# Block-sparse attention and a gated feed-forward on one Trainium2 core: the written order of arithmetic changed past the third pair of ff tiles of batch 0

## The chip, the cores and the metric

The kernel runs on one core of one Trainium2 chip, in one launch. The core has five engines that work side by side, each through its own list of instructions in order: TensorE (PE, matmuls; its weight loads are shown apart as PEld), VectorE (DVE), ScalarE (ACT), GpSimd (POOL) and SyncE (SP). POOL and SP here also issue the transfers between HBM and the on-chip memories: loads of q, k, v and the weights go out on POOL's queue, stores, DMA transposes and small on-chip copies on SP's. The metric is the device time in microseconds of one execution; less is better.

## The reference

Two stages, one behind the other. The first is attention with a band and block summaries: q, k and v have 4 batches of 8 heads of 768 rows of 64. The second is a gated feed-forward on the 3072 x 512 result.

```python
k_sum = k.reshape(B, H, 24, 32, D).max(axis=3)      # one key per block of 32
v_sum = v.reshape(B, H, 24, 32, D).mean(axis=3)
scores_l = q @ k.T / 8                              # only where |i - j| < 16
scores_s = q @ k_sum.T / 8 + log(32)                # all 24 blocks
a = softmax(concat([scores_l masked, scores_s]))
x = a @ concat([v, v_sum])                          # -> 3072 x 512
h = x @ w_in                                        # 512 x 2048
out = (h * sigmoid(1.702 * h)) @ w_out              # 2048 x 512
```

Inputs and output are float32.

## The kernel before

**Tiles.** A batch is 768 tokens. Its eight heads are four pairs (a pair fills 128 partitions), its tokens two halves of 384. Attention works on pairs; the feed-forward's first product makes 16 tiles of 128 ff rows for each half, its second three pieces of 128 rows for each half, and these by seven block products in place of eight, from sums of the GELU's outputs (`gs`) and of the weights (`ws`).

**What sets the order.** Nothing is left to a scheduler. A long string, `ORDER` (lines 35 to 111), holds 1,002 words `name.arguments`; lines 932 to 934 look each word up in `ops` (line 916) and call it, in the order of the string. A wrapper, `_Ordered` (lines 18 to 32), keeps the instructions of each engine in that program order, which is why every instruction bears line 28 in the profile. So a word fixes the place of its instructions on their engine, and the engines are tied together only by the semaphores that the tiles' reads and writes call for. An instruction that waits holds back all that follow it on its engine, DMA issues on POOL and SP among them.

**The words that matter here.**

- Loads on POOL: `lk`, `lq`, `lv` (a pair's keys or queries, a part of the values), into `kb`, `qb` and `vw`. `gate.b` (line 910) is a small POOL copy that holds the loads behind it until the block sums of the batch before have landed in `vw`, or, for the last batch, the turned `x`.
- Keys and queries of batch 1: `tk`, `tq` turn them on PE (`ps_t`), `kc`, `qc` copy them out, `kh` copies the neighbours' rows (halos), `xm` takes the block maxima, `kr` puts them in rows of `kx`. Batches 2 and 3 are turned by DMA transposes on SP instead (`xk`, `xq`), and then `xa` (maxima of two pairs, DVE), `ka` (line 420, halos, POOL or DVE) and `kR` (line 428, maxima into rows of `kx`, DVE) follow.
- Attention: `s.b.half.p` scores into a pair of PSUM banks (PE, `ps_s`), `e` exp (ACT), `m` the mask (DVE), `vm` the block sums of the values on PE, `vb` (line 373) the same on DVE, `sd` and `ha` (lines 345 and 336) copies of the sums and halos into `vw` on SP, `v` the values (PE, `ps_av`), `nn` the division (DVE, `x`). `t` and `c` turn `x` on PE and copy it; in later batches `d` does it by a DMA transpose on SP.
- Feed-forward: `f.half.nt.kos.bank` (line 722) one ff tile of 4 matmuls into a PSUM bank (`ph`), `g` (line 738) its GELU on ACT, which frees the bank; `gs.j.n.what` (line 741) the sums of GELU outputs, on DVE or with `.g` on POOL; `ws` (line 819) the same of weights; `p.t.what.bank` (line 830) one product of 8 matmuls (`poA`, `poB`, `poC`); `x.t.what` (line 853) takes it from the bank by a copy or an addition into an output buffer (`osb`); `o.b.t.half` (line 870) the store on SP. `G` and `X` load ACT's tables for GELU and for exp.

**Buffers.** There are eight PSUM banks: 0 to 3 for ff tiles, products and sums, and 4 and 5 of two banks each, named by halves (40, 41, 50, 51). There are three output buffers `osb`: a fourth piece can be started only when a store has landed. `vw`, `kx` and `qT` have two sets each.

**Stages.** While the ff tiles of batch b run on PE and the GELU on ACT, keys and values of batch b+1 come in and are made ready; the products of batch b then stand between the scores, exps and values of batch b+1. Half 1 of an ff tile needs all tokens of half 1, so the ff stage of a batch begins with the tiles whose tokens are ready.

Of the kernel before, what the change touches and what calls it, by code (L numbers as in the profile page):

```python
# [43 lines left out]
f.0.2.k0123.1 s.0.1.3.42 e.1.3 f.0.1.k23 f.0.4.k0123.50 mf f.0.6.k0123.40 f.0.5.k0123.51 f.0.7.k0123.41 G  # L44
f.0.3.k0123.0 g.0.2 g.0.0 g.0.1 g.0.4 g.0.6 g.0.3 lk.1.3 lq.1.0 g.0.7 g.0.5 lq.1.3 ck.1 m.1.0 m.1.2 ow.1 lk.1.4 lk.1.1
lk.1.2 lv.1.5.1 lk.1.5 lk.1.6 lq.1.2 lk.1.7 m.1.1 lq.1.1 lv.1.0.0 lq.1.4 lq.1.5 lq.1.7 lv.1.3.1 lq.1.6 lv.1.0.1
lv.1.2.0 lv.1.1.0 cv.1 lv.1.1.1 lv.1.4.0 lv.1.2.1 f.0.8.k0123.2 lv.1.4.1 late m.1.3 ws.0.0 g.0.8 f.0.9.k0123.3
# [35 lines left out]
o.1.2.0.0.2 p.2.4 x.2.4.a f.0.1.k01.0 f.0.9.k01.3 f.0.0.k01.2 f.0.0.k23 xk.1.1.0 xk.1.0.1 f.0.8.k01.1 f.0.8.k23
f.0.1.k23 lv.3.5.1 lq.3.1 lq.3.2 g.0.0 g.0.8 g.0.1 o.1.1.1.0.2 f.0.9.k23 g.0.9 xk.1.1.1 xk.1.0.0 o.1.2.1.0.2 xq.1.1
f.1.0.k0123.2 g.1.0 f.1.8.k0123.1 g.1.8 f.1.1.k0123.0 xq.1.0 g.1.1 gs.0.2.2 f.1.9.k0123.3 g.1.9 f.0.2.k0123.2 g.0.2
f.1.2.k0123.1 g.1.2 f.0.10.k0123.0 gs.0.2.0.d gs.0.2.1 gs.0.2.3 g.0.10 f.1.10.k0123.3 g.1.10 xa.0.1 f.1.3.k0123.1
f.0.3.k0123.2 g.0.3 f.1.11.k0123.3 f.0.11.k0123.0 g.1.3 gs.2.2.2.g g.0.11 g.1.11 ka.1.d gs.2.2.0 f.0.12.k0123.1
ha.3.3.0 f.0.4.k0123.2 gs.2.2.1.g g.0.12 g.0.4 f.1.12.k0123.3 ha.3.1.0 g.1.12 vm.3.52 f.1.4.k0123.0 vb f.1.14.k0123.3
g.1.14 sd.3.1.0 f.0.5.k0123.2 g.1.4 ha.3.0.0 ha.3.2.0 xa.1.1 gs.2.2.3 kR.1.d g.0.5 f.1.5.k0123.1 f.1.13.k0123.3 g.1.5
g.1.13 f.0.13.k0123.0 gs.4.2.0 gs.4.2.2 g.0.13 gs.4.2.1 gs.4.2.3 f.0.6.k0123.2 g.0.6 f.1.6.k0123.1 g.1.6  # L90
f.0.14.k0123.0 g.0.14 gs.6.1.0 gs.6.1.2 gs.6.1.1 gs.6.1.3 sd.3.0.0 f.0.7.k0123.2 g.0.7 f.1.7.k0123.1 g.1.7
f.0.15.k0123.0 g.0.15 f.1.15.k0123.3 g.1.15 gs.7.1.0 p.0.1.2 x.0.1.d p.0.5.1 gs.7.1.1.g s.3.0.0.52 X s.3.0.1.42 e.0.1
# [872 lines left out]
```

## Time and profile before

| | |
|---|---|
| runs of before, us | 212.35, 213.48, 214.64; median 213.48 |
| the profiled execution, us | span 212.3; its own time is not listed apart from this span |
| PE busy | 199.1 (94%), 2440 matmuls |
| DVE, ACT, POOL busy | 127.8 (60%), 117.7 (55%), 108.6 (51%) |
| granted PE clock | full in all 40 slices |
| POOL's queue / SP's queue, share of the 16 DMA engines | 85.7% / 31.9% |
| chain that ended last | PE 72%, DMA 18%, POOL 4%, issue 2%, DVE 1% |

The span counts from the first to the last recorded event of one execution. A group of instructions is named output<-input by the program's tiles, so `ph<-xT,w_in_sb` is an ff tile, `poA`, `poB` and `poC` are products, `ps_s` scores, `ps_av` values, `ps_t` turns and `gT<-ph` the GELU. A row of the timeline gives start, duration, engine, operation, tiles and shapes, the number of instructions drawn together, and in brackets the idle time ahead with what ended it. A row of the waits gives engine, tile, what released it, then total idle us, number of times and the longest in us. A row of the chain gives start, duration, engine, tile and number of instructions. A row of the windows gives the stretch, its length, then for each engine the busy time and the number of instructions: PE, PEld, DVE, ACT, POOL; behind them the granted clock, the DMA share and GB/s. A row of the DMA issues gives tiles, queue, operation, count, size and the median time from issue to landing.

### The profile page before, as it was taken

To read this page: it belongs to the slowest core of one execution; us is meant where nothing else is said; L and a number is where in the kernel's file an instruction comes from. 1 tells how busy PE (TensorE), PEld (TensorE's weight loads), DVE (VectorE), ACT (ScalarE), POOL (GpSimd) and SP (SyncE) were. 2 spreads that over 40 slices of the span, in tenths; PEclk is the share of its full clock that TensorE was granted. 3 is DMA by queue.
4 is the path that set the end of the run, shared out by engine and by line. 5 is a ranking of instruction groups with operands and counts; after the bars stand their busy time and mean duration, and the time that the engine had idled before them with its cause. 6 is when DMAs were issued, how large, how long until landed. Compare 5 with 4: busy or idle time off the path is not lost.

```text
span 212.3 us, 5885 instructions
## 1 busy us (share of the span) xinstructions
PE 199.1 (94%) x2440; PEld 145.3 (68%) x2440; DVE 127.8 (60%) x311; ACT 117.7 (55%) x227; POOL 108.6 (51%) x157
## 2 busy tenths in 40 slices
...
PEclk9999999999999999999999999999999999999999
...
GB/s 69 156 166 190 209 218 216 178 135 123 98 138 203 111 160 179 120 164 170 145 153 201 134 220 128 253 171 59 3 99 60 181 112 0 0 3 0 99 102 99
DMA packets 96458, 27.74 MB, mean 131 GB/s; under 512 B 85024, under 2 KB 93488, under 8 KB 96432
## 3 DMA queue, kind: packets, MB, share of 16 engines
q0 software_dynamic: 70800, 13.64, 85.7%
q1 hardware_dynamic: 25632, 13.74, 31.9%
...
## 4 chain that ended last, share of the span: by engine, by line
PE 72%; DMA 18%; POOL 4%; issue 2%; DVE 1%; SPq 0%; POOLq 0%
PE ph L28 31%; PE poA L28 19%; PE poB L28 9%; DMA w_out_sb<-in_moe_w_out_dram 7%; PE poC L28 5%; DMA kb<-in_k_dram 4%; DMA v0n<-in_v_dram 4%; DMA vw<-vs 3%; PE ps_av L28 3%; PE ps_s L28 2%; PE ps_t L28 1%; POOL kb L28 1%; PE ps_vs L28 1%; DVE vs L28 1%; POOL mk L28 1%
## 5 line engine op out<-in xcount | busy, mean ns | idle before, releaser
L28 PE MATMUL ph<-xT,w_in_sb 128*128 128x384 f16 x512 | 85.9, 326 | 0.0
L28 ACT ACTIVATE gT<-ph 128x384 f16<-128x384 f32 x128 | 58.7, 495 | 22.9 <-PE ph L28 21.9
L28 PEld LDWEIGHTS <-w_in_sb 128*128 128x128 f16 x512 | 49.2, 98 | 31.5 <-DMA w_in_sb<-in_moe_w_in_dram 0.2
L28 PEld LDWEIGHTS <-gs 128*128 128x128 f16 x384 | 36.3, 98 | 4.7
L28 DVE TENSOR_TENSOR gs<-gT 128x768 f16<-128x768 f16 (+1 forms) x36 | 17.1, 490 | 21.5 <-ACT gT L28 21.4
L28 PEld LDWEIGHTS <-gT 128*128 128x128 f16 x288 | 27.5, 98 | 3.7
L28 ACT ACTIVATE a_sb<-ps_s 128x768 bf16<-128x768 f32 x32 | 24.5, 808 | 9.1 <-PE ps_s L28 9.0
...
L28 PE MATMUL poA<-ws,gs 128*128 128x256 f16 x192 | 24.9, 273 | 0.0
L28 POOL TENSOR_TENSOR gs<-gT 128x768 f16<-128x768 f16 x4 | 6.9, 1728 | 35.0 <-ACT gT L28 35.0
L28 ACT ACTIVATE s<-poA 128x256 f32<-128x256 f32 x14 | 5.4, 384 | 20.6 <-PE poA L28 19.0
L28 DVE TENSOR_TENSOR x<-ps_av,rc 128x768 f16<-128x768 f32 (+1 forms) x18 | 15.6, 869 | 0.6
L28 DVE TENSOR_TENSOR a_sb<-a_sb,mk 128x768 bf16<-128x768 bf16 x28 | 14.6, 549 | 1.8 <-ACT a_sb L28 1.1
L28 POOL TENSOR_TENSOR gs<-gs,gT 128x768 f16<-128x768 f16 (+1 forms) x6 | 8.4, 1406 | 12.9 <-DVE gs L28 12.9
L28 DVE TENSOR_TENSOR gs<-gT,gs 128x768 f16<-128x768 f16 (+1 forms) x19 | 9.2, 490 | 7.2 <-POOL gs L28 6.6
L28 PE MATMUL poB<-ws,gs 128*128 128x256 f16 x96 | 12.5, 273 | 0.0
L28 PE MATMUL poB<-w_out_sb,gs 128*128 128x256 f16 x96 | 12.5, 273 | 0.0
L28 PE MATMUL poA<-ws,gT 128*128 128x256 f16 x96 | 12.5, 273 | 0.0
L28 PE MATMUL poC<-w_out_sb,gT 128*128 128x256 f16 x96 | 12.5, 273 | 0.0
L28 PE MATMUL poA<-w_out_sb,gT 128*128 128x256 f16 x96 | 12.3, 273 | 0.0
...
## 6 DMA issues: line engine op xcount, KB each, us to landing
out_dram<-osb SPq DMA_DIRECT2D x23, 256.0 KB, 2.9
...
```

Source lines behind the costliest of these rows:

```text
L28: r = f(*a, **kw)
```

## The change

Only the `ORDER` string differs. Its 1,002 words are the same, in another sequence, and the two strings are equal up to `g.0.11`, the GELU of ff tile 11 of half 0 in batch 0; `v.0.1.2.50` follows soon in both, and what comes behind it is in another order. Loads on POOL's queue keep their sequence among each other, as do the transfers on SP's, but for one store at the end; the arithmetic between them has moved, so a given load or store can stand ahead of an instruction that it stood behind before. Bank and engine are part of a word, so over the whole string each is used as often as before.

The core of the diff, by stage. Second half of the ff tiles of batch 0 with the keys of batch 1, and the first products:

```diff
...
-c.1.1.d f.1.0.k01.2 f.1.8.k01.3 f.1.1.k0123.1 ws.1.0 g.0.15 g.1.1 f.1.0.k23 ws.2.0 f.1.8.k23 g.1.0 g.1.8 ws.0.1 ws.1.1
-f.1.9.k0123.0 g.1.9 gs.0.2.0 ws.3.0 gs.0.2.1 gs.0.2.3 f.1.10.k0123.1 gs.0.2.2 ws.2.1 g.1.10 f.1.2.k0123.3 g.1.2
-f.1.3.k0123.2 g.1.3 f.1.11.k0123.1 g.1.11 gs.2.2.0 gs.2.2.1 gs.2.2.2 f.1.12.k0123.3 gs.2.2.3 g.1.12 f.1.4.k0123.2
-tk.0.52 kc.0.a f.1.13.k0123.0 g.1.13 ws.3.1 g.1.4 f.1.5.k0123.1 g.1.5 tk.1.52 gs.4.2.2 kc.1.a f.1.14.k0123.3 tk.2.42
...
-s.1.1.1.52 e.1.1 m.0.1 vm.1.42 vb sd.1.1.0 kr.2.1.g kh.3.1.d sd.1.0.0 xm.3.1 kr.3.1.d p.1.5.1 gate.1 lv.2.3.0 lv.2.1.1
...
-lq.2.7 o.0.1.0.0.2 v.1.0.0.50 m.1.3 v.1.0.1.51 p.1.4 x.1.4.a o.0.1.1.0.2 p.2.5.1 x.2.5.a m.0.3 v.1.1.0.40 v.1.1.1.41
...
+v.0.1.3.51 nn.1.1 f.0.15.k0123.0 g.0.12 f.0.14.k0123.1 g.0.13 t.1.1.52 c.1.0.d c.1.1.d g.0.15 ws.0.1 g.0.14 f.1.8.k01.3
+f.1.0.k01.2 f.1.8.k23 ha.1.3.0 f.1.9.k0123.0 f.1.0.k23 ws.1.1 g.1.8 g.1.9 f.1.1.k0123.1 ws.2.0 f.1.2.k0123.3 g.1.0
+f.1.3.k0123.2 g.1.1 ws.1.0 gs.0.2.0 ha.1.2.0 f.1.10.k0123.1 g.1.3 gs.0.2.1 f.1.4.k0123.2 g.1.2 gs.2.2.2 g.1.10 lv.1.5.0
+gs.0.2.3 f.1.11.k0123.1 g.1.4 f.1.12.k0123.3 g.1.11 f.1.13.k0123.0 ws.3.1 tk.0.52 g.1.13 gs.2.2.0 g.1.12 kc.0.a
...
+p.0.4 vb sd.1.1.0 x.0.4.a gate.1 s.1.1.1.52 e.1.1 lv.2.3.0 p.1.5.1 kr.3.1.d x.1.5.d x.1.2.a m.1.0 x.1.6.a s.1.0.2.52
+sd.1.0.0 p.2.1.2 m.0.1 x.2.1.a p.1.3 s.1.0.3.42 o.0.0.1.0.2 p.1.7 lv.2.1.1 e.0.2 m.1.1 lk.2.0 e.0.3 s.1.1.2.52 lk.2.2
+lv.2.2.0 x.1.7.a x.1.3.a lv.2.2.1 lk.2.3 p.2.6 e.1.2 lv.2.5.1 s.1.1.3.42 m.0.2 p.1.4 v.1.0.0.50 e.1.3 v.1.0.1.51 lk.2.1
...
```

The ff tiles of batch 1 with the keys of batch 2, and its products:

```diff
...
-f.0.13.k0123.0 g.0.13 f.1.13.k0123.3 g.1.5 f.0.6.k0123.2 vm.2.42 g.1.13 g.0.6 gs.4.2.0 gs.4.2.2.d vb sd.2.0.0
...
-g.1.7 f.0.15.k0123.0 ha.2.3.0 g.0.15 gs.6.1.1 f.0.7.k0123.1 g.0.7 kR.0.d f.1.15.k0123.3 g.1.15 gs.7.1.0 X gs.6.1.3
-p.0.1.2 s.2.0.1.52 e.0.1 s.2.0.0.42 lv.3.1.0 lk.3.0 lk.3.4 lv.3.1.1 lk.3.2 gs.7.1.1 lk.3.7 lk.3.3 ha.2.1.0 x.0.1.d
...
-x.1.3.a o.1.1.0.0.2 nn.0.1 d.0.1 p.2.1.2 x.2.1.d p.1.4 v.2.1.0.40 v.2.1.1.41 nn.1.0 x.1.4.d v.2.1.2.50 v.2.1.3.51
...
+f.0.13.k0123.0 f.1.15.k0123.3 g.0.5 f.0.6.k0123.2 g.1.5 g.0.13 lv.3.1.1 g.1.15 vm.2.42 f.0.14.k0123.0 gs.2.2.0 ka.0.g vb
...
+g.1.13 f.1.7.k0123.2 f.1.14.k0123.3 lv.3.4.1 f.0.7.k0123.1 g.1.7 xa.1.0 gs.7.1.0 sd.2.0.0 kR.0.d g.0.15 lv.3.0.1
+sd.2.1.0 g.1.14 gs.4.2.0 p.0.2.0 s.2.0.0.42 gs.6.1.0 ha.2.0.0 g.0.7 gs.7.1.2 s.2.0.1.52 lv.3.5.0 gs.4.2.1 X lv.3.2.0
...
+lq.3.7 m.1.0 p.1.4 p.2.1.2 v.2.1.0.40 v.2.1.2.50 d.0.0 v.2.1.1.41 v.2.1.3.51 x.2.5.a x.2.1.d x.1.3.a lq.3.3 p.2.6
+o.1.1.0.0.2 x.1.4.d d.0.1 p.2.3 nn.1.0 x.2.6.a p.2.7 nn.1.1 p.2.2.3 x.2.7.a x.2.2.a lv.3.4.0 d.1.0 lv.3.2.1 p.2.4
+f.0.9.k01.3 x.2.3.a f.0.1.k01.0 G d.1.1 o.1.2.0.0.2 f.0.1.k23 f.0.8.k01.1 f.0.8.k23 f.0.9.k23 x.2.4.a f.0.0.k01.2
...
```

Batches 2 and 3 are re-ordered in the same manner, and the end of the string:

```diff
...
-p.2.1.2 x.2.1.d p.2.5.1 x.2.5.a p.2.6 x.2.6.d p.2.2.0 x.2.2.a p.2.7 x.2.7.a o.3.2.1.1.2 p.2.3 x.2.3.a o.3.2.0.0.2
-p.2.4 x.2.4.d P7.0 o.3.1.1.0.2 o.3.2.1.0.1
+o.3.1.0.0.2 p.2.5.1 p.2.7 x.2.5.a p.2.3 x.2.7.a p.1.4 p.2.4 x.2.3.a x.1.4.d x.2.4.d o.3.2.1.1.2 o.3.2.0.0.2 P7.0
+o.3.1.1.0.2 o.3.2.1.0.1
...
```

More of the change, by code (lines that the diff above doesn't have):

```diff
@@ L43 @@
 sd.0.0.3 ha.0.2.3 sd.0.1.3 ha.0.3.3 ha.0.0.3 lk.1.0 f.0.0.k23 ha.0.1.3 Qc.1.3.d s.0.1.2.52 f.0.1.k01.3 e.1.2
[L44 to L47, printed above, removed]
@@ L83 @@
[L83 to L87, printed above, removed]
@@ L88 @@
[L88 to L92, printed above, removed]
@@ new lines @@
+lk.1.5 lk.1.6 lq.1.2 lk.1.7 m.1.1 lq.1.1 lv.1.0.0 lq.1.4 lq.1.5 lq.1.7 lv.1.3.1 lq.1.6 lv.1.0.1 lv.1.2.0 lv.1.1.0 cv.1
+lv.1.1.1 lv.1.4.0 lv.1.2.1 f.0.8.k0123.2 lv.1.4.1 late m.1.3 ws.0.0 g.0.8 f.0.9.k0123.3 f.0.11.k0123.0 g.0.9
+f.0.10.k0123.1 v.0.1.0.40 v.0.1.1.41 lv.1.3.0 nn.1.0 g.0.11 g.0.10 v.0.1.2.50 f.0.13.k0123.3 f.0.12.k0123.2 t.1.0.42
+v.0.1.3.51 nn.1.1 f.0.15.k0123.0 g.0.12 f.0.14.k0123.1 g.0.13 t.1.1.52 c.1.0.d c.1.1.d g.0.15 ws.0.1 g.0.14 f.1.8.k01.3
+f.1.0.k01.2 f.1.8.k23 ha.1.3.0 f.1.9.k0123.0 f.1.0.k23 ws.1.1 g.1.8 g.1.9 f.1.1.k0123.1 ws.2.0 f.1.2.k0123.3 g.1.0
@@ new lines @@
+qc.1.a gs.6.1.3 lv.2.0.0 tq.2.42 p.1.1.3 qc.2.a gs.7.1.1 gs.4.2.3 p.0.5.1 x.0.5.a p.0.6 tq.3.52 kr.0.1.d s.1.0.0.42
+x.0.6.a x.0.2.a gs.7.1.2 X gs.7.1.3 kr.1.1.d x.1.1.d xm.3.1 kh.2.1.g p.1.2.0 e.0.0 p.0.3 p.0.7 lq.2.3 m.0.0 x.0.3.a
+x.0.7.a kh.1.1.d qc.3.d s.1.1.0.42 e.1.0 p.1.6 xm.2.1 vm.1.42 o.0.0.0.0.2 s.1.0.1.52 lv.2.5.0 e.0.1 kr.2.1.g kh.3.1.d
+p.0.4 vb sd.1.1.0 x.0.4.a gate.1 s.1.1.1.52 e.1.1 lv.2.3.0 p.1.5.1 kr.3.1.d x.1.5.d x.1.2.a m.1.0 x.1.6.a s.1.0.2.52
+sd.1.0.0 p.2.1.2 m.0.1 x.2.1.a p.1.3 s.1.0.3.42 o.0.0.1.0.2 p.1.7 lv.2.1.1 e.0.2 m.1.1 lk.2.0 e.0.3 s.1.1.2.52 lk.2.2
@@ new lines @@
+lv.2.2.0 x.1.7.a x.1.3.a lv.2.2.1 lk.2.3 p.2.6 e.1.2 lv.2.5.1 s.1.1.3.42 m.0.2 p.1.4 v.1.0.0.50 e.1.3 v.1.0.1.51 lk.2.1
+m.0.3 m.1.3 lk.2.4 v.1.1.0.40 v.1.1.1.41 x.2.6.a p.2.5.1 G lk.2.5 nn.0.0 nn.1.0 x.2.5.a lk.2.7 p.2.7 o.0.1.0.0.2
+t.0.0.52 lk.2.6 x.2.7.a x.1.4.a p.2.2.3 t.1.0.42 p.2.3 x.2.2.a c.0.0.a c.1.0.a m.1.2 lv.2.1.0 v.1.0.2.50 lq.2.1
+v.1.0.3.51 v.1.1.2.40 x.2.3.a v.1.1.3.41 p.2.4 f.0.1.k01.0 nn.0.1 t.0.1.52 nn.1.1 lv.2.0.1 c.0.1.d o.0.1.1.0.2 lq.2.4
+lv.2.3.1 x.2.4.a o.0.2.0.0.2 f.0.9.k01.3 f.0.8.k01.1 f.0.0.k01.2 lv.2.4.0 t.1.1.42 c.1.1.d f.0.1.k23 g.0.1 f.0.8.k23
@@ new lines @@
+f.0.0.k23 g.0.8 g.0.0 f.0.9.k23 o.0.2.1.0.2 g.0.9 lq.2.6 lv.2.4.1 xk.0.0.0 lq.2.5 f.1.1.k0123.0 f.1.0.k0123.2 lq.2.7
+g.1.0 xk.0.0.1 g.1.1 f.1.8.k0123.1 lv.3.1.0 xk.0.1.0 g.1.8 xk.0.1.1 f.1.9.k0123.3 f.0.2.k0123.2 g.1.9 g.0.2
+f.1.2.k0123.1 lk.3.0 f.1.10.k0123.3 g.1.2 f.0.10.k0123.0 f.1.3.k0123.1 xq.0.0 gs.0.2.0 g.1.10 g.1.3 g.0.10
+f.1.11.k0123.3 f.0.3.k0123.2 f.0.11.k0123.0 g.1.11 g.0.3 f.1.12.k0123.3 gs.0.2.2.d xq.0.1 g.0.11 gs.0.2.1.g
+f.0.4.k0123.2 f.1.4.k0123.1 g.0.4 xa.0.0 f.0.12.k0123.0 g.1.4 f.0.5.k0123.2 f.1.5.k0123.1 g.0.12 lk.3.4 g.1.12
@@ new lines @@
+gs.6.1.2.d gs.6.1.3 ha.2.1.0 s.2.0.3.52 gs.4.2.2.d e.0.2 e.0.3 gs.0.2.3 p.1.5.0 p.0.6 gs.4.2.3 gs.2.2.2.d s.2.1.0.42
+s.2.1.1.52 x.0.6.a lk.3.1 p.0.3 p.0.7 e.1.0 x.0.3.a lv.3.3.0 m.0.3 lq.3.0 p.1.1.3 x.0.7.a e.1.1 lq.3.4 m.0.1 s.2.1.3.52
+m.0.2 s.2.1.2.42 x.1.1.a e.1.3 e.1.2 p.0.4 p.1.6 lv.3.0.0 x.0.4.a v.2.0.0.40 x.1.6.a v.2.0.2.50 v.2.0.1.41 x.1.5.d
+v.2.0.3.51 m.1.2 p.1.2.2 m.1.1 lq.3.5 p.1.7 o.1.0.0.0.2 nn.0.0 x.1.2.a o.1.0.1.0.2 m.1.3 x.1.7.a p.1.3 nn.0.1 lv.3.3.1
+lq.3.7 m.1.0 p.1.4 p.2.1.2 v.2.1.0.40 v.2.1.2.50 d.0.0 v.2.1.1.41 v.2.1.3.51 x.2.5.a x.2.1.d x.1.3.a lq.3.3 p.2.6
@@ new lines @@
+o.1.1.0.0.2 x.1.4.d d.0.1 p.2.3 nn.1.0 x.2.6.a p.2.7 nn.1.1 p.2.2.3 x.2.7.a x.2.2.a lv.3.4.0 d.1.0 lv.3.2.1 p.2.4
+f.0.9.k01.3 x.2.3.a f.0.1.k01.0 G d.1.1 o.1.2.0.0.2 f.0.1.k23 f.0.8.k01.1 f.0.8.k23 f.0.9.k23 x.2.4.a f.0.0.k01.2
+f.0.0.k23 lk.3.6 g.0.1 g.0.9 g.0.8 f.1.1.k0123.0 f.1.8.k0123.1 g.0.0 f.1.9.k0123.3 g.1.1 g.1.9 g.1.8 f.1.0.k0123.2
+f.0.10.k0123.0 g.0.10 gate.2 g.1.0 gs.0.2.2 xk.1.1.0 f.1.2.k0123.1 gs.0.2.0.d gs.0.2.1 xk.1.0.1 f.1.10.k0123.3 g.1.2
+o.1.1.1.0.2 g.1.10 lq.3.6 f.0.2.k0123.2 gs.0.2.3 lv.3.5.1 f.1.3.k0123.1 vm.3.52 g.1.3 xk.1.1.1 g.0.2 xk.1.0.0
@@ new lines @@
+o.1.2.1.0.2 f.0.13.k0123.0 f.0.3.k0123.2 f.1.11.k0123.3 f.0.12.k0123.1 g.0.3 g.0.13 g.1.11 xa.0.1 f.0.4.k0123.2 xq.1.1
+f.1.12.k0123.3 lq.3.1 f.0.11.k0123.0 g.0.4 gs.2.2.2.g g.0.12 f.1.5.k0123.1 g.0.11 lq.3.2 vb xa.1.1 xq.1.0 f.0.5.k0123.2
+g.1.5 g.1.12 ha.3.3.0 f.1.4.k0123.0 kR.1.d g.1.4 f.1.14.k0123.3 g.0.5 f.1.6.k0123.1 g.1.14 gs.2.2.0 ha.3.1.0
+f.0.14.k0123.0 gs.2.2.1.g f.0.6.k0123.2 g.1.6 f.1.13.k0123.3 g.0.14 f.1.7.k0123.1 f.0.15.k0123.0 g.1.13 g.0.6 ka.1.d
+f.1.15.k0123.3 f.0.7.k0123.2 s.3.0.1.42 gs.2.2.3 g.1.7 gs.6.1.0 gs.6.1.1 g.1.15 gs.4.2.0 g.0.15 gs.6.1.3 s.3.0.0.52
@@ new lines @@
+sd.3.1.0 g.0.7 gs.6.1.2 p.0.2.3 gs.7.1.0 p.0.1.2 X ha.3.0.0 e.0.1 p.1.2.0 e.0.0 x.0.1.d m.0.1 gs.7.1.1.g p.0.5.1
+s.3.0.2.52 e.0.2 gs.4.2.1 x.0.5.d s.3.0.3.42 e.0.3 p.0.6 x.0.2.a gs.4.2.2 p.1.1.3 x.0.6.d s.3.1.1.42 gs.7.1.2 gs.7.1.3
+s.3.1.0.52 gs.4.2.3 e.1.0 p.0.7 x.1.1.d p.0.3 ha.3.2.0 e.1.1 m.0.2 s.3.1.3.42 e.1.3 s.3.1.2.52 p.1.6 x.1.2.a x.0.3.a
+m.0.0 x.0.7.a m.1.3 m.0.3 sd.3.0.0 p.1.5.1 v.3.0.2.40 e.1.2 v.3.0.0.50 v.3.0.3.41 v.3.0.1.51 o.2.0.0.0.2 G x.1.6.a m.1.2
+p.0.4 p.1.7 m.1.0 x.0.4.a nn.0.0 x.1.5.d m.1.1 x.1.7.a p.2.1.2 p.1.3 nn.0.1 o.2.0.1.0.2 x.2.1.d p.1.4 d.0.0 v.3.1.2.40
@@ new lines @@
+v.3.1.3.41 x.1.3.a v.3.1.0.50 v.3.1.1.51 x.1.4.d d.0.1 p.2.5.1 p.2.6 nn.1.0 nn.1.1 x.2.6.a o.2.1.0.0.2 x.2.5.d p.2.2.3
+x.2.2.a p.2.7 x.2.7.a p.2.3 p.2.4 f.0.1.k01.0 x.2.4.a f.0.1.k23 f.0.9.k01.3 f.0.0.k01.2 x.2.3.a f.0.9.k23 f.0.8.k01.1
+f.0.0.k23 f.0.8.k23 o.2.1.1.0.2 g.0.9 g.0.0 g.0.8 d.1.0 d.1.1 f.1.9.k0123.3 f.1.0.k0123.2 g.0.1 f.1.8.k0123.1
+f.1.1.k0123.0 g.1.9 g.1.0 f.0.2.k0123.2 f.1.11.k0123.3 g.1.8 g.0.2 f.1.2.k0123.1 g.1.1 f.0.10.k0123.0 g.1.11
+f.1.13.k0123.3 g.1.2 f.1.3.k0123.1 g.0.10 f.0.3.k0123.2 g.1.13 f.1.10.k0123.3 g.0.3 f.0.11.k0123.0 f.0.4.k0123.2 g.1.3
@@ new lines @@
+g.1.10 f.1.12.k0123.3 o.2.2.0.0.2 gs.2.2.0.d g.0.4 g.0.11 f.1.4.k0123.1 gs.2.2.1.g g.1.12 f.0.12.k0123.0 f.1.14.k0123.3
+o.2.2.1.0.2 g.0.12 gs.0.2.0.d f.0.5.k0123.2 g.1.4 f.1.5.k0123.1 f.0.13.k0123.0 g.0.5 f.0.6.k0123.2 gs.2.2.2.g g.1.5
+g.0.13 g.1.14 f.1.6.k0123.1 f.0.14.k0123.0 g.0.6 g.1.6 gs.6.1.0.d f.0.7.k0123.2 g.0.7 gs.0.2.2.g gs.4.2.0.g
+f.1.7.k0123.1 g.0.14 f.1.15.k0123.3 g.1.7 gs.0.2.1.g f.0.15.k0123.0 gs.4.2.1 g.0.15 gs.6.1.1 gs.6.1.2.d gs.2.2.3 p.0.1.2
+g.1.15 gs.7.1.0 gs.7.1.1.g p.0.5.1 x.0.1.d p.0.2.0 p.0.6 x.0.6.a x.0.2.a gs.6.1.3 gs.4.2.2.d x.0.5.d gs.7.1.2 p.1.1.3
```

54 lines of the change are left out of this document (11 added, 43 removed).

## The prediction, made before the changed kernel was run

> **What bounds the kernel now.** First the page, for the busy shares; then the waits of TensorE (PE), for where it stands still; then the chain that ended last, for what each piece of PE's work costs.
>
> ```profile
> span 212.3 us, 5885 instructions
> PE 199.1 (94%) x2440; PEld 145.3 (68%) x2440; DVE 127.8 (60%) x311; ACT 117.7 (55%) x227; POOL 108.6 (51%) x157
> PEclk9999999999999999999999999999999999999999
> ```
> ```profile
> PE ps_s L28 <- issue: 1.8, 1, 1.8
> PE ps_av L28 <- DMA vw<-vs: 1.3, 1, 1.3
> PE ps_t L28 <- DMA kb<-in_k_dram: 0.6, 1, 0.6
> ```
> ```profile
> 51.55 1.75 PE poA L28 x16
> 81.05 14.62 PE ph L28 x90
> 103.52 0.70 PE ps_s L28 x24
> 106.94 0.46 PE ps_s L28 x24
> 207.71 0.89 PE poA L28 x8
> ```
>
> PE is busy 94% of the span at full granted clock. The change neither adds nor removes a matmul, so it can only move PE's idle time. One product (`p`, 8 matmuls) is 1.75/16 x 8 = 0.87 us, one ff tile (`f`, 4 matmuls) 14.62/90 x 4 = 0.65 us, a pair of score blocks (`s`) 0.46 us. Behind the point where the orders part, PE stands still four times: 0.6 us at the first turn of batch 1's keys, 1.3 us before `v.1.0.0`, 1.8 us before the first scores of batch 2, and that pair takes 0.70 instead of 0.46, 0.24 more. That is 4.0 us, all that a new order can win before the tail; whatever it starves is lost.
>
> **The change part by part.** Operations and counts are the same on every engine; the sums run from this execution's span. Its own time is not listed apart from the span; what lies around it (the lowest listed run, 212.35, is as good as the span, the median 1.2 above) I take as unchanged.
>
> *First wait, 45.8 us.* The turn `tk.0` waits for a load:
>
> ```profile
> 45.80 0.51 PE L28 MATMUL ps_t<-wide,kb 128*128 128x128 bf16 x6 [0.61 <-DMA kb<-in_k_dram]
> 44.57 0.49 ACT L28 ACTIVATE gT<-ph 128x384 f16<-128x384 f32 x1 [0.16 <-PE ph L28]
> ```
>
> Eleven ff tiles of half 1 now stand ahead of `tk.0`, not ten: 0.65 us, which covers 0.61. Against it, several `f` follow the GELU that frees their PSUM bank more closely (`f.1.4` right behind the bank's `g.1.3`, the first product behind `g.1.15`); a GELU of 0.49 that starts 0.16 behind its tile leaves up to 0.1 each, in some three places 0.3. Net -0.3.
>
> *Second wait, 69.6 us.* `v.1.0.0` needs the block sums that the sync queue copies (`sd`):
>
> ```profile
> 41.53 0.69 DVE L28 TENSOR_TENSOR ws<-w_out_sb,ws 128x1024 f16<-128x1024 f16 x1 [0.46 <-DMA w_out_sb<-in_moe_w_out_dram]
> 61.56 0.29 DVE L28 COPY vpart<-ps_vs 128x128 f32<-128x128 f32 x1 [0.87 <-PE ps_vs L28]
> 61.89 1.18 DVE L28 TENSOR_TENSOR vs<-ps_vs,vpart 32x128 bf16<-32x128 f32 x4
> 62.46 0.66 SPq L28 DMA_DIRECT2D out_dram<-osb  x1
> 63.22 1.25 SPq L28 DMA_DIRECT2D vw<-vs  x2
> 68.60 0.42 DVE L28 TENSOR_TENSOR osb<-poC,s 128x256 f32<-128x256 f32 x1 [1.27 <-DMA out_dram<-osb]
> 69.63 0.64 PE L28 MATMUL ps_av<-vw,a_sb 128*64 128x65 bf16 x24 [1.32 <-DMA vw<-vs]
> 69.11 0.43 POOL L28 COPY gate<-vw 32x1 bf16<-32x1 bf16 x1 [6.67 <-DMA vw<-vs]
> ```
>
> The sums end at 61.89+1.18 = 63.07 and the queue itself is free at 62.46+0.66 = 63.12, so two limits fall together. The landing gives the time, not PE: the change puts 16 products before `v.1.0.0` where 14 stood, 1.74 us of cover, and without a wait PE would arrive at 68.3-0.3+1.74 = 69.75. Two things work against that. DVE now begins its half-1 work with `ws.0.1 ws.1.1`, and `ws.1.1` waits for the load that ended at 41.5; `ws.2.0 ws.1.0` and the first `gs` queue behind it. Before, DVE did those two sums of 0.69 ahead of that load and stood only 0.46 for it; now they come behind, so up to 1.4 more stands empty. With the key steps of head pair 3 also moved ahead of `vb`, adding DVE's rows from 41.5 I put the end of the sums at about 63.7, 0.5 late. And the third output buffer now goes to `x.1.2`, so `x.1.7` is the one that waits for the first store (68.6 in the row above), with `p.1.4` behind it: PE at 68.6+0.42 for `p.1.4`, then 0.87 and the hand-overs, `v.1.0.0` at 70.05. That is later than the landing at 69.6 to 70.1, which hides. Lead: 1.74-(70.05-69.63) = **1.3 us** (bounds 0.8, a landing 0.5 later still, to 1.75). If the sums are late without that cover, each us passes to PE, and, through `gate`, to every load of batch 2.
>
> *Third wait, 101.7 us.*
>
> ```profile
> 96.11 1.75 DVE L28 TENSOR_REDUCE ka<-kx 128x48 bf16<-128x1536 bf16 x1 [1.76 <-DMA kx<-kb]
> 96.14 1.61 POOL L28 COPY kx<-kx 128x320 bf16<-128x320 bf16 x3 [5.67 <-DMA kx<-kb]
> 97.69 0.71 POOL L28 DMA_DIRECT2D vw<-in_v_dram  x1
> 98.39 0.84 POOL L28 DMA_DIRECT2D kb<-in_k_dram  x1
> 100.76 1.18 DVE L28 TENSOR_TENSOR vs<-ps_vs,vpart 32x128 bf16<-32x128 f32 x4
> 103.11 0.52 DVE L28 COPY kx<-ka 128x576 bf16<-128x576 bf16 x2
> 101.73 1.78 issue
> ```
>
> The chain says "issue", but scores read `kx`, and the row that ends there is `kR.0`, key sums copied at 103.11; PE starts at 103.52 between its two halves (hence 0.70). DVE had the maxima (`xa.1.0`) at 97.86 and did five `gs`, `vb` and three more `gs` first. The new order has `vb` ahead of `xa.1.0` and one 0.35 us `gs` between `xa.1.0` and `kR.0`. `vb` ends near 96.5, two `gs` follow, `xa.1.0` ends about 99.2, `kR.0` by 100.0. PE, 1.3 us ahead, arrives at 101.73-1.3 = 100.4. On POOL the halos `ka.0` now stand behind two more issues, `lk.3.4` (which waits for the same landing) and `lv.3.1.1`: 96.14+0.84+0.71, plus 1.61, ends at 99.3. Both fit, by half a microsecond. I keep 0.2 of the 2.0 as left (bounds 0 and 0.5, those slacks used up by loads that now run beside the transposes). Lead **3.1**.
>
> The transposes' own price:
>
> ```profile
> kx<-kb SPq DMA_TRANSPOSE x4, 7.7
> qT<-qb SPq DMA_TRANSPOSE x2, 6.2
> qT<-qb SPq DMA_TRANSPOSE x1, 5.2
> ```
>
> The last one lands 5.2 us after its issue, with no load beside it; those beside loads took 7.7. `lv.3.1.0` and `lk.3.0` now go out beside it. [...] At 7.7 the landing would be 2.5 later, at 103.5, where `s.2.0.2` arrives about 103.6: hidden still, just.
>
> *After that.* DVE defers six `gs` into the products of batch 1, and `p.0.3` follows `gs.0.2.3` with nothing to spare: +0.2 (0 to 0.5, one 0.55 us `gs`). ff of batch 2 is the larger place:
>
> ```profile
> 117.58 0.42 DVE L28 TENSOR_TENSOR osb<-poB,s 128x256 f32<-128x256 f32 x1 [0.27 <-PE poB L28]
> 119.11 0.53 SPq L28 DMA_DIRECT2D out_dram<-osb  x1
> 124.13 0.41 DVE L28 TENSOR_TENSOR osb<-poC,s 128x256 f32<-128x256 f32 x1
> 125.44 12.35 PE ph L28 x76
> out_dram<-osb SPq DMA_DIRECT2D x1, 256.0 KB, 4.8
> xT<-x SPq DMA_TRANSPOSE x3, 5.1
> ```
>
> Before, the store `o.1.1.0` left 6.3 us ahead of the ff tiles and landed 4.8 later, which frees the buffer for `x.2.2`, whose bank the first tile takes. Now `x.1.3` comes behind `x.2.1`, and the store leaves only some 4.3 us ahead: 4.8 plus `x.2.2`'s 0.41 overshoot by 0.9. The transpose `d.0.1`, behind that store on SP, lands in the same stretch. +0.8 (0, if the loads have thinned out, to 1.0). Lead 2.1. In batches 2 and 3 I followed each PSUM bank to the GELU or copy that frees it and found none late.
>
> *Tail.* The built order of SP is the same but for one store: `o.3.1.1` (256 KB) stood ahead of the last three and is now last but one, since `x.1.4` comes behind `x.2.3`.
>
> ```profile
> out_dram<-osb SPq DMA_DIRECT2D x2, 128.0 KB, 1.7
> out_dram<-osb SPq DMA_DIRECT2D x1, 256.0 KB, 2.0
> 208.62 0.42 DVE L28 COPY osb<-poA 128x256 f32<-128x256 f32 x1 [0.45 <-PE poA L28]
> ```
>
> It leaves 0.7 us ahead of the last store, and takes 2.0 where that takes 1.7; +0.2 (0 to 0.5). **Sum**: 3.1-0.2-0.8-0.2 = 1.9 us off: 213.48-1.9 = **211.6 us** (the profiled span 210.4). Its own range, from the bounds, is 0.3 to 3.6 us off, 209.9 to 213.2.
>
> **The rivals.**
> *The slack holds everywhere.* For it: the two late places rest on DMA times of a crowded stretch, and elsewhere a 256 KB store took 2.0. Then 1.75+2.0 less a little: 3.6 off, 209.9.
> *The transfers take the gain back.* Batch 2's keys hang on `gate`, 69.11, and PE can't score before they land. Should loads beside them put the landing of `kx` 2 us later, `lk.3.4` and with it `ka.0` end at 101.3, the lead there is 2.0 and the rest eats 1.2: 0.8 off, 212.7. For it: 7.7 against 5.2. Against: only two loads come earlier.
> *Slower: DVE falls behind in the first products.* The place is 41.5 to 64 us, where
>
> ```profile
> 40.00:50.00 10.00, 9.38 (x70) 5.89 (x69) 9.11 (x18) 7.85 (x16) 8.15 (x11) 1.00 2.12 139
> 50.00:60.00 10.00, 10.00 (x132) 8.37 (x130) 9.16 (x26) 7.90 (x15) 10.00 (x15) 1.00 1.64 103
> ```
>
> DVE (third column) is busy 9.1 and 9.2 of 10 and has little room for 1.4 us of waiting. The price is one for one: `p.0.5`, `p.0.6` and `s.1.0.0` follow their `gs` and key rows within 0.3 by my sum, and `vb`, `sd`, `gate` and all of batch 2 come after. From 2 us of slip on, the 1.9 is gone. The new order also puts six to eight `gs` among the first products of each later batch, so the same can recur: with 2 us here and one DVE `gs` of 0.49 plus its queueing, say 0.7, in each of the three later batches, 4.1 are lost against 1.9: 2.2 slower, 215.7. Against: DVE waited 0.9 for PE before `vb`, so some slack is there.
> *The order does not do what it says*: transfers are kept, but their times hang on waits that the arithmetic sets. If the queue's waits fix the pace, all moves end inside 0.3: 213.5.
>
> **How the numbers follow.** Forecast 0.45, slack holds 0.10, transfers 0.15, slower 0.25, nothing 0.05. 1% (2.1 us) is about what a measurement of this kernel tells from no change: its three runs lie 2.3 apart. Faster by over 1% (under 211.3): somewhat under half of the forecast (0.20), the slack case (0.10), a little of the transfers (0.03): 0.33. Slower by over 1% (above 215.6): the half of the slower case in which DVE loses 4 us or more, and a little of the transfers: 0.15. Same: 0.52. The range reaches to the slack case and to where the slower one has its middle, 209.8 to 215.6.
>
> **What would show it.** Right: `ps_t` no longer waits for `kb`; `ps_av` waits under 0.5 for `vs`; the first scores of batch 2 start at 100 to 101 with 0.46 a pair; a wait of about 0.8 at the first ff tiles of batch 2; PE's last product ends about 206.5. Wrong: `ps_s` or poB waiting for DVE before 64; `vb` ending past 64.5; scores still held by `kx`, through POOL; idle PE in batch 3.

## The result and the profile after

The changed kernel takes 212.06 us (median of 22 runs, 210.3 to 214.35), the kernel before on the same chip 212.83 (22 runs, 210.93 to 214.9). The ratio is **0.995, with a 95% interval of 0.9927 to 0.9974**: 1.1 us faster, 0.6 to 1.6. That is inside the 1% that I called no change, and a little over half of the 1.9 us that I forecast. (The ratios, here and below, compare undisturbed runs alone; medians and ranges count every run.)

The page of the changed kernel, its first rows and the granted clock:

```profile
span 210.0 us, 5880 instructions
PE 200.4 (95%) x2440; PEld 145.8 (69%) x2440; DVE 130.8 (62%) x311; ACT 114.3 (54%) x227; POOL 109.1 (52%) x157
PEclk9999999999999999999999999999999999999998
```

The waits of PE of the same kernel (total, times, longest, us), those of the lead-in left out:

```profile
PE ps_s L28 <- issue: 0.4, 1, 0.4
PE ph L28 <- DVE osb L28: 0.4, 1, 0.4
```

The waits for `kb` (0.6), for the sums `vs` (1.3) and most of the 1.8 ahead of batch 2's scores are gone, and one new one of 0.4 stands at the ff tiles of batch 2. The span is 2.3 us shorter, more than the runs say. PE's busy time rose from 199.1 to 200.4. Most of that is not the new order's doing: in the first 34 us, where the two orders are the same, PE was busy 28.8 us in this profile of before and 29.6 in that of the changed kernel, and the second profile of before, below, has 29.5 there too. Behind 34 us the rise is 0.5 (0.7 between the second profiles). A part can be read from the chain of the changed kernel, where the same product costs 0.87 behind another product and 0.98 behind scores:

```profile
59.27 0.87 PE poA L28 x8
60.14 0.28 PE ps_s L28 x12
60.42 0.98 PE poA L28 x8
```

Behind the point where the orders part, 20 products of the old string stand directly behind scores or values, and 22 of the new. A tenth of a microsecond each is a price that I had not put on any edit, but it makes only 0.2 of the 0.5.

### The profile page after: what moved, and what is told of

It reads as the page before. It is cut to its first block, busy times and chain, and to the rows that moved or that the text cites. A ratio compares the mean times of both kernels' runs of the same rounds, so it can differ in the third digit from the quotient of the medians.

```text
span 210.0 us, 5880 instructions
## 1 busy us (share of the span) xinstructions
PE 200.4 (95%) x2440; PEld 145.8 (69%) x2440; DVE 130.8 (62%) x311; ACT 114.3 (54%) x227; POOL 109.1 (52%) x157
## 4 chain that ended last, share of the span: by engine, by line
PE 79%; POOL 12%; DMA 5%; issue 1%; DVE 1%; SPq 0%; POOLq 0%; DVEq 0%
PE ph L28 36%; PE poA L28 19%; PE poB L28 10%; PE poC L28 5%; PE ps_s L28 3%; PE ps_av L28 3%; DMA vw<-vw 2%; POOL mk L28 2%; DMA out_dram<-osb 2%; POOL v0n L28 2%; POOL w_in_sb L28 2%; POOL kb L28 2%; POOL kx L28 2%; POOL qb L28 1%; PE ps_t L28 1%
## 5 line engine op out<-in xcount | busy, mean ns | idle before, releaser
L28 ACT ACTIVATE gT<-ph 128x384 f16<-128x384 f32 x128 | 56.1, 495 | 30.6 <-PE ph L28 29.9
L28 DVE TENSOR_REDUCE ka<-kx 128x48 bf16<-128x1536 bf16 x4 | 7.0, 1750 | 7.4 <-DMA kx<-kb 7.4
```

The source lines that it names most:

```text
L28: r = f(*a, **kw)
```

## The experiments

**Both kernels a second time.** One profile each is little to read a difference of half a percent from.

> The kernel before, unchanged, profiled a second time. The two profiles differ by 2.3 us of span (212.3 and 210.0), the medians by 0.77. Theory A (PE's four idle times are a property of the order): idle times of 0.6, 1.3, 1.8 again, 3.9 us in all past 33 us, within 0.4. Theory B (the profiled execution of before was one with late transfers): the waits of v.1.0.0 for the block sums and of the first scores of batch 2 come out shorter, 2.6 us in all or less, and the span is near 211.

> The changed kernel, unchanged, profiled a second time. Both theories: no wait before v.1.0.0, 0.3 to 0.6 us before the first scores of batch 2, 0.2 to 0.6 us before the first ff tile of batch 2, span 209 to 211. If idle times here vary by over 1 us from the first profile, what one profile shows of a transfer wait can't be carried to the median.

The waits of PE of the kernel before, second execution:

```profile
span 212.6 us, 5885 instructions
PE ps_av L28 <- DMA vw<-vs: 1.4, 1, 1.4
PE ph L28 <- DMA xT<-x: 1.3, 1, 1.3
PE ps_s L28 <- issue: 0.9, 1, 0.9
```

And of the changed kernel, second execution, two rows of the waits and the two places on the timeline:

```profile
span 211.7 us, 5880 instructions
PE ph L28 <- DVE osb L28: 1.4, 1, 1.4
PE ps_av L28 <- DMA vw<-vw: 1.4, 2, 0.9
...
112.47 0.92 PE L28 MATMUL ps_av<-vw,a_sb 128*64 128x65 bf16 x47 [0.93 <-DMA vw<-vw]
...
124.78 3.41 PE L28 MATMUL ph<-xT,w_in_sb 128*128 128x384 f16 x20 [1.45 <-DVE osb L28]
```

Neither theory holds as it was put. The kernel before loses as much as the first time, but not in the same places: the scores' wait is half as long, and the ff tiles of batch 2 wait 1.3 for a turned `x`. The changed kernel has two waits that its first profile hid or showed small: the first values of batch 2 wait 0.9 for the halo copies in `vw`, and the first ff tile 1.45 for the output buffer. Its span is above the 209 to 211 that I expected. Between the second profiles lie 0.9 us, between the first 2.3.

**Each half of the change alone.** The two orders hold the same words, so one can take the new sequence for the words of batch 0's stage and keep the old one behind it, or the reverse. The diffs here and below show only the words around each change.

```diff
@@ newold, against before @@
-g.0.11 lv.1.5.0 g.0.10 v.0.1.2.50 v.0.1.3.51
+g.0.11 g.0.10 v.0.1.2.50 f.0.13.k0123.3
...
-p.2.4 t.0.1.52 f.0.1.k01.0 nn.1.1 x.2.4.a o.0.2.1.0.2
+x.2.4.a o.0.2.0.0.2 lv.2.4.0 o.0.2.1.0.2 lq.2.6 lv.2.4.1 lq.2.5 lq.2.7
 f.0.8.k01.1 f.0.9.k01.3 c.0.1.d f.0.0.k01.2 G f.0.0.k23
...
@@ oldnew, against after @@
-g.0.11 g.0.10 v.0.1.2.50 f.0.13.k0123.3
+g.0.11 lv.1.5.0 g.0.10 v.0.1.2.50 v.0.1.3.51
...
-c.0.1.d o.0.1.1.0.2 lq.2.4 lv.2.3.1 x.2.4.a o.0.2.0.0.2
+p.2.4 t.0.1.52 f.0.1.k01.0 nn.1.1 x.2.4.a c.0.1.d G
 f.0.9.k01.3 f.0.8.k01.1 f.0.0.k01.2 lv.2.4.0 t.1.1.42
...
```

> The new order for all words that the order of before has up to the last store of batch 0's first pieces (the words of its batch 0 stage), the order of before for the rest. It keeps the gains at the first and second waits, and loses those of the third. Theory A: idle 0.6 and 1.3 go, 0.5 comes back as closely followed GELUs, so PE is about 1.1 us ahead at the ff tiles of batch 1, and the third wait keeps its 1.8 since VectorE and the transposes move ahead with PE: 1.1 us faster than before (ratio 0.995). Rival: the third wait is set by the landing of the transposed keys, and these by the loads, not by PE: PE arrives earlier and waits longer, and the gain is under 0.4 us (ratio over 0.998).

> The other half alone: the order of before for the words of the batch 0 stage, the new order from the ff tiles of batch 1 on. The first two waits, 0.6 and 1.3, stay. Theory A: the third goes from 2.0 to 0.4 and the ff tiles of batch 2 wait 0.4, so 1.2 us faster than before (ratio 0.994). Theory B: the third wait is shorter in most executions than in the profiled one, and the gain is 0.3 to 0.6 us (ratio 0.997 to 0.999).

The new first stage alone: ratio 1.0041 (1.0002 to 1.008), no gain and if anything slower, as the rival had it. The new rest alone: 0.9963 (0.9932 to 0.9993), which lies between its two theories and is most of the whole gain. Why the first half is worth nothing by itself is in VectorE's timeline: the maxima of the second pair of keys (`ka<-kx`) and the copy of the maxima into the score rows (`kx<-ka`, `kR.0`). First in the second profile of before:

```profile
94.94 1.75 DVE L28 TENSOR_REDUCE ka<-kx 128x48 bf16<-128x1536 bf16 x1 [0.62 <-DMA kx<-kb]
...
101.93 0.52 DVE L28 COPY kx<-ka 128x576 bf16<-128x576 bf16 x2
```

Then in `newold`, with the scores that wait for it:

```profile
95.56 1.75 DVE L28 TENSOR_REDUCE ka<-kx 128x48 bf16<-128x1536 bf16 x1 [1.50 <-DMA kx<-kb]
...
102.55 0.52 DVE L28 COPY kx<-ka 128x576 bf16<-128x576 bf16 x2
...
99.43 1.04 PE L28 MATMUL poA<-w_out_sb,gT 128*128 128x256 f16 x8
102.96 0.94 PE L28 MATMUL ps_s<-qT,kx 64*128 64x64 bf16 x24 [2.49 <-issue]
```

And in the changed kernel, from the block sums on:

```profile
94.88 0.29 DVE L28 COPY vpart<-ps_vs 128x128 f32<-128x128 f32 x1 [0.75 <-PE ps_vs L28]
...
98.20 1.74 DVE L28 TENSOR_REDUCE ka<-kx 128x48 bf16<-128x1536 bf16 x1
...
100.13 0.77 DVE L28 COPY kx<-ka 128x576 bf16<-128x576 bf16 x2
```

With the old list, `kR.0` starts 7.0 us behind the start of `xa.1.0`, which waits for a transpose: 103.11-96.11 in the first profile of before, 101.93-94.94 in the second, 102.55-95.56 in `newold`. So the end of the wait follows the landing and not PE, and a PE that comes earlier waits longer (2.49). In the changed kernel `xa.1.0` has no idle time in front of it; the last thing that VectorE waited for is PE's own block sums, and `kR.0` starts 5.25 us behind those (5.15 in its second profile, where `xa.1.0` did not wait either). The change ties `kR.0` to PE's pace where it was tied to the transposes.

That a lead from the first stage then carries to the end is argued, not shown: the whole change, 0.995, and its second half alone, 0.9963, can't be told apart. Nor did the first stage's waits stay in the profile of `oldnew` as I had expected. PE did not wait for `kb` there and only 0.53 us for `vs`, and it came to batch 2's first scores at 100.4, as in the changed kernel. In the four profiles with the old first stage the wait for `vs` was 1.32, 1.42, 0.53 and 0.54; in all ten with the new one there was none.

`newold` is not only not faster; it also shows a low clock. The windows of PE (stretch, length, busy and count, granted clock, DMA share, GB/s):

```profile
102.00:103.00 1.00, 0.04 (x2) 0.83 3.38 122
103.00:106.00 3.00, 3.00 (x35) 0.50 2.15 161
106.00:107.00 1.00, 1.00 (x11) 0.97 1.79 190
```

**One word moved.** If the place of `kR.0` is what counts, moving it alone should do.

```diff
@@ oldkr, against before; newoldkr, the same against newold @@
-g.0.12 ka.0.g f.1.5.k0123.1
+g.0.12 ka.0.g kR.0.d f.1.5.k0123.1
...
-f.0.7.k0123.1 g.0.7 kR.0.d f.1.15.k0123.3
+f.0.7.k0123.1 g.0.7 f.1.15.k0123.3
```

> The order of before with one word moved: the copy of batch 2's key maxima into the score rows, kR.0, comes right behind the halos ka.0, ahead of five gs and of vb on VectorE. In three profiles with the old list it stood 7.0 us of VectorE's own work behind the landing of the last key transpose, and the scores waited for it by 1.8, 0.9 and 2.5 us. Theory C (that list, not the first stage, is what the change is worth): kR.0 ends near 100, the wait goes, and this alone is as good as the whole change, 1.0 to 1.4 us off, ratio 0.994. Rival: the work that kR.0 passes is needed as early, the wait moves to p.0.5 or to the values, and the gain is under 0.4 us, ratio over 0.998.

> The kernel with the new batch 0 stage and the old rest, with kR.0 moved in the same way. Theory C: the 1.1 us that the new first stage gains on PE were lost in the third wait, which VectorE's list held at a fixed distance from the transposes; with the wait gone they stay, and the ratio to before is 0.989 (1.3 and 1.1 us). Rival: what the first stage gains is lost elsewhere too (PE's closer following of GELUs, a later transpose): the same time as with the old first stage and kR.0 moved, 0.994, or slower.

`oldkr`: ratio 1.0006 (0.9972 to 1.004), no gain. `newoldkr`: 0.9974 (0.9931 to 1.0016), against `newold`'s 1.0041; it rests on 7 of 12 runs, and the median of all 12 is no better than that of before (213.59 against 213.04). Theory C falls for the first. VectorE's and PE's timeline of `oldkr`:

```profile
98.86 0.91 DVE L28 COPY kx<-ka 128x576 bf16<-128x576 bf16 x2
100.63 0.28 DVE L28 COPY vpart<-ps_vs 128x128 f32<-128x128 f32 x1
100.95 1.18 DVE L28 TENSOR_TENSOR vs<-ps_vs,vpart 32x128 bf16<-32x128 f32 x4
...
102.18 0.35 PE L28 MATMUL ps_s<-qT,kx 64*128 64x64 bf16 x12 [1.13 <-DVE vs L28]
...
104.69 1.87 PE L28 MATMUL poA<-ws,gs 128*128 128x256 f16 x8 [0.70 <-DVE s L28]
```

`kR.0` ends at 99.8 as foreseen, but `s.2.0.0` takes PSUM bank 42, where `vm.2.42` put the block sums, and `vb` frees it only at 102.1. Two waits stood one behind the other, and I had seen the later one. (The profiled execution of `oldkr` took 215.03, 1.9 us above the median of its runs; what else it shows may not be typical.) The change moves both, `vb` ahead of `xa.1.0` and `kR.0` behind it. In the profile of `newoldkr` the wait is gone, but there the transposes also landed early (`xa.1.0` at 92.6), so that one profile doesn't show by itself that the first stage's lead was kept, and the intervals of `newold` and `newoldkr` overlap a little.

**Mending the waits that are left.** Two sums moved behind `kR.0`; then also the store that frees the output buffer, earlier; then also the halo copies, earlier.

```diff
@@ fixkeys, against after @@
-f.0.15.k0123.0 gs.2.2.3 lk.3.5
+f.0.15.k0123.0 lk.3.5
...
-xa.1.0 gs.7.1.0 sd.2.0.0 kR.0.d g.0.15
+xa.1.0 sd.2.0.0 kR.0.d gs.7.1.0 g.0.15
...
-gs.6.1.1 x.0.1.d
+gs.6.1.1 gs.2.2.3 x.0.1.d
@@ fixboth, against fixkeys @@
-x.2.5.a x.2.1.d x.1.3.a lq.3.3 p.2.6 o.1.1.0.0.2
+x.2.5.a x.1.3.a o.1.1.0.0.2 x.2.1.d lq.3.3 p.2.6
@@ after_ha, against after; fixha, the same against fixboth @@
-xq.0.1
+ha.2.2.0 ha.2.0.0 ha.2.3.0 ha.2.1.0 xq.0.1
...
```

> The changed kernel with two sums moved behind kR.0 on VectorE: gs.7.1.0 (0.35 us) right behind it, gs.2.2.3 (1.0 us there, beside POOL's copies) behind gs.6.1.1. kR.0 ends about 1.3 us earlier, at 99.5 in the first profile's time, PE arrives at 100.4: the 0.4 us ahead of the first scores of batch 2 goes, ratio to before 0.993 where the changed kernel has 0.995. Rival: the halos ka.0 on POOL end at 99.0 and may slide; the wait then only changes its name, and the ratio stays at 0.995.

> As the one before, and x.1.3 of batch 1 ahead of x.2.1 on VectorE, with its store o.1.1.0 ahead too. The store leaves about 1.0 us earlier and frees the buffer for x.2.2 earlier by as much: the wait ahead of the first ff tile of batch 2, 0.4, 0.4 and 1.45 us in three profiles, is 0 to 0.5. Ratio to before 0.990. Rival: the landing of stores is set by the loads beside them, not by when they leave: the wait stays, and the time is that of the kernel without this second edit.

> The changed kernel with the four halo copies of batch 2's values (ha.2.*) ahead of the last query transpose xq.0.1 on the sync queue, where that queue stands idle from 92.7 to 95.7 us. Theory E (the halo copies are what is late once the scores no longer wait): in three profiles the last of them landed at 110.9, 112.3 and 112.1 us, and the first values of batch 2, due at 111.9, 111.3 and 110.6, waited 0, 0.9 and 1.5. Here they land before 105, no value waits, and the ratio to before is 0.993 where the changed kernel has 0.995. Rival: the copies ahead of xq.0.1 push its landing from 103.2 past 104, and s.2.0.2 waits for queries what the values waited before: the ratio stays or gets worse.

> All three edits on the changed kernel: two sums behind kR.0, x.1.3 and its store ahead of x.2.1, the halo copies ahead of xq.0.1. Theory E: no idle time of PE over 0.5 us behind 46 us, span 208.5 to 209.5, ratio to before 0.988 to 0.990. Rival: with each wait gone the next transfer takes its place (queries, the turned x for the ff tiles of batch 2), and the ratio is that of fixkeys, 0.992.

`fixkeys`: 0.9923 (0.9884 to 0.9962). `fixboth`: 0.9929 (0.9882 to 0.9976). `after_ha`: 1.0024 (0.999 to 1.0059). `fixha`: 0.9982 (0.9948 to 1.0016). The scores and the first ff tile of `fixkeys`, then the first values and the first ff tile of `fixboth`, and one row of the waits each of `after_ha` and `fixha`:

```profile
99.60 0.62 DVE L28 COPY kx<-ka 128x576 bf16<-128x576 bf16 x2
100.73 0.52 PE L28 MATMUL ps_s<-qT,kx 64*128 64x64 bf16 x24
...
122.33 5.85 PE L28 MATMUL ph<-xT,w_in_sb 128*128 128x384 f16 x35
```
```profile
112.22 0.92 PE L28 MATMUL ps_av<-vw,a_sb 128*64 128x65 bf16 x47 [1.46 <-DMA vw<-vw]
...
123.16 5.04 PE L28 MATMUL ph<-xT,w_in_sb 128*128 128x384 f16 x30 [0.20 <-DVE osb L28]
```
```profile
PE ps_s L28 <- DMA qT<-qb: 3.0, 1, 3.0
```
```profile
PE ps_s L28 <- DMA qT<-qb: 3.5, 1, 3.5
```

The keys' wait goes, as expected. What the earlier store does is not shown: the wait for the output buffer is 0.2 in `fixboth`, but `fixkeys`, without that edit, has none at all. The halo copies differ in the same way. PE came to batch 2's values at 110.8 in `fixboth` and found them not landed (1.46); in `fixkeys` it came at 111.7 and did not wait. Sending these ahead of the last query transpose removes that wait and makes a larger one, 3.0 and 3.5 us for queries: the rival of `after_ha` holds. `fixkeys` and `fixboth` can't be told from the changed kernel by their intervals: 0.9923 and 0.9929 against 0.995. In the three profiles that still have a wait of over 1 us it ends with a transfer that was issued and landed between 92 and 113 us. So I take the room on the DMA engines there, and not an order of instructions, to be what stands in the way of the rest; no run made that stretch lighter, and this is not shown.

**A longer wait.**

```diff
@@ latekr, against after @@
-xa.1.0 gs.7.1.0 sd.2.0.0 kR.0.d g.0.15
+xa.1.0 gs.7.1.0 sd.2.0.0 g.0.15
...
-p.0.2.0 s.2.0.0.42 gs.6.1.0 ha.2.0.0 g.0.7 gs.7.1.2 s.2.0.1.52
+p.0.2.0 gs.6.1.0 g.0.7 gs.7.1.2 gs.4.2.1 gs.7.1.1 gs.7.1.3 kR.0.d s.2.0.0.42 ha.2.0.0 s.2.0.1.52
...
```

> The changed kernel with six words (five sums, 2.5 us of VectorE, and a GELU) between xa.1.0 and kR.0 that stood behind it. The wait ahead of the first scores of batch 2 grows from 0.4 to about 2.9 us. Theory F (PE pays the wait one for one, and a wait of over 2 us costs more, since PE's granted clock falls to half for 3.3 us, as it did in the profile of newold where 11 products and tiles lost 1.1 us): 2.5 us and some 1.1 to 1.5 for the clock over the changed kernel, ratio to before 1.012 to 1.015, and the profile shows 0.5 in the clock behind the wait. Rival: the low clock in newold was chance and not the wait's doing: 2.5 us only, ratio 1.007, clock full.

Ratio 1.0043 (1.0 to 1.0086). The sums took less time than I had counted, and the wait is 2.15:

```profile
101.97 0.69 PE L28 MATMUL ps_s<-qT,kx 64*128 64x64 bf16 x24 [2.15 <-issue]
...
102.00:103.00 1.00, 1.00 (x28) 1.00 1.26 199
103.00:106.00 3.00, 3.00 (x48) 1.00 1.96 185
...
25.00:26.00 1.00, 1.00 (x18) 0.50 1.22 207
```

The wait grew by 1.7 us, and 1.0043-0.995 of 212.8 is 2.0: about one for one, though the intervals allow 0.9 to 3.0, so that a further price of about a microsecond is not excluded. The clock stayed full behind this wait, so the second part of theory F isn't shown here. The same profile lists a mean clock of 0.991, and its low stretch is the last row: it lies in the lead-in, where no edit reaches, and ended at about 26.1 us (the clock was 0.95 from 26 to 27 us and 1.00 behind). So the mean granted clock that is listed with each run does not tell where it was low. It is 0.992 or less in 8 of 12 runs of `latekr` and 8 of 12 of `newold`, the two kernels with the longest single wait for `kR.0`, in 5 of 12 each of `after_ha` and `fixha`, whose waits of 3.0 and 3.5 us are longer still, in 24 of 87 of before, 3 of 22 of the changed kernel and none of 12 of `oldnew`. Whether a long wait makes a low clock likelier stays open.

**A sum on the other engine.**

```diff
@@ gsdve, against after @@
-xq.0.1 g.0.11 gs.0.2.1.g f.0.4.k0123.2
+xq.0.1 g.0.11 gs.0.2.1.d f.0.4.k0123.2
```

> The changed kernel with one sum of batch 1, gs.0.2.1, on VectorE instead of GpSimd. In the changed kernel gs.2.2.0 on VectorE took 1.71 us, where such a sum takes 0.55 elsewhere, all of it beside that GpSimd sum. Theory G (two-input operations of the two engines hold each other up): gs.2.2.0 takes 0.55 here; the sums beside the halo copies ka.0 keep 0.75 and 1.0. VectorE waits for PE's block sums right behind, so the time is that of the changed kernel, 0.993 to 0.998. Rival: gs.2.2.0 is slow for another reason (it waits for its GELU inside the operation): it keeps 1.7.

The changed kernel, VectorE and GpSimd:

```profile
92.06 1.65 POOL L28 TENSOR_TENSOR gs<-gs,gT 128x768 f16<-128x768 f16 x1
92.42 1.71 DVE L28 TENSOR_TENSOR gs<-gT 128x768 f16<-128x768 f16 x1
```

The same sum in `gsdve`:

```profile
91.97 0.55 DVE L28 TENSOR_TENSOR gs<-gT 128x768 f16<-128x768 f16 x1
```

Theory G holds: 0.55 without the GpSimd sum beside it, 1.71 with it. The ratio, 0.9895 (0.9846 to 0.9944), rests on only 3 runs; its interval overlaps that of the changed kernel, and its profiled span is 210.5 against 210.0. That it is faster than the changed kernel is not shown.

## Why the prediction was right or wrong

**The sign was right, the time lay in the range, and the change is under 1%, which I had called the likeliest; the gain was too large by 0.8 us.** The range says little: it is 5.8 us wide, and the runs of either kernel spread over 4. That the forecast, 211.6, lies within 0.5 of the measured 212.06 is partly luck, since the median that it started from, 213.48, was 0.65 too high.

*Baseline: wrong.* I took the lowest listed run to be "as good as the span". The profiled runs of the changed kernel took 211.7 for a span of 210.0 and 213.44 for 211.7, so 1.7 us lie around the span, and the profiled execution of before, 212.3, was one of about 214.0, above the median of 212.83. I subtracted waits of an execution above the median from a median.

*First wait: the cause was right, the gain was not there.* `kb` is not waited for. But from batch 0's values on, where PE had waited for halo copies, to `tk.0` the old order took 45.80-34.38 = 11.42 and the new one 46.68-34.69 = 11.99, of which 0.65 is the further tile: 0.1 gained, not 0.3. `oldnew`, which has the old order there and did not wait for `kb`, took 10.63. So what I had put at 0.3 against the gain, the tiles that follow their GELUs closely, came to some 0.7; what these are made of no run shows.

*Second wait: right in size, wrong in cause.* Lead 1.3 was forecast with `v.1.0.0` at 70.05. In the chain of the changed kernel the products run through without an idle step to 69.39+0.98 = 70.37. By the prediction's own sum the lead is then 1.74-(70.37-69.63) = 1.0, and 1.3 with the lead-in, which ended 0.3 later in this execution. `x.1.7` did not wait for a store, as I had it; it started at 67.89, as its product ended. `vb` ended at 62.83+1.18 = 64.0 where I had 63.7. VectorE stood 0.50 us for the weights' load, not up to 1.4 more than before. The landing of the sums, which I had taken over from before, was not the same: their two copies took 3.0 and 4.2 us where they had taken 5.7 and 5.8, and `gate` ran at 67.04 where it ran at 69.11. So the landing was hidden, by more than I thought; why the copies were quicker no run shows.

```profile
62.83 1.18 DVE L28 TENSOR_TENSOR vs<-ps_vs,vpart 32x128 bf16<-32x128 f32 x4
67.89 0.42 DVE L28 TENSOR_TENSOR osb<-poA,s 128x256 f32<-128x256 f32 x1 [1.23 <-PE poA L28]
69.39 0.98 PE poA L28 x8
```

*Third wait: the mechanism was right* (`kR.0` behind other work in VectorE's list, `vb` moved ahead). `kR.0` by 100.0 was forecast; it ran from 100.13 to 100.90, the scores started at 100.8 after 0.43 us, and PE's arrival at 100.4 was met. **The term was mis-sized**: 1.8 of 2.0 us were to go. Between the first profiles 1.4 went, since 0.43 of wait was left and the first pair still took 0.66 in place of 0.46; between the second, where before had lost only 0.9 and 0.24, it was 0.6. Nor was the lead of 3.1 a sum of two independent gains of 1.3 and 1.8: in `newold` the first is worth nothing while `kR.0` hangs on the transposes. The two halves alone multiply to 1.000 where the whole is 0.995, a difference as large as its uncertainty.

*After that: one wait missed, one under-sized.* I had named only `p.0.3` among the products of batch 1, and followed PSUM banks further on; the halo copies that the values of batch 2 read I did not follow. They cost 0 in one profile and 0.9 in the other, 1.46 in `fixboth`. The ff tiles of batch 2 were given 0.8 with 1.0 as the upper end; they waited 0.4 and 1.45. The cause was right: in the chain of the changed kernel the store stands ahead of them, with a copy into the output buffer between.

```profile
118.16 4.38 DMA out_dram<-osb
...
123.10 8.61 PE ph L28 x52
```

`p.0.3` waited for nothing.

*Tail: nothing.* From PE's last product to the end of the span 3.7 us lay before and 3.6 lie now.

*The rivals.* DVE falling behind in the first products did not come. The transfers taking the gain back is nearest to what happened, though by the halo copies and a store, not by the keys' transposes that I priced: `xa.1.0`, which waits for those in the old order, did not wait in either profile of the changed kernel.
